# SSM forward and FFN gate/up of one training step: from one after the other to one interleaved phase

## The chip, the cores and the metric

The kernel runs on 1 core of one Trainium2 chip, in one launch. The metric is the device time of that core in microseconds (us), the median of 3 runs.

## The reference

One block, forward and backward, in bfloat16, L = 2048 positions, D = 576 channels, N = 128 states per channel, F = 4608 hidden units:

```python
xn = layernorm(x)                       # [2048, 576]
K  = Re(sum_n C*dt*B * exp(dt*A*l))     # one kernel of 2048 taps per channel
s  = irfft(rfft(xn) * rfft(K)) + xn * Dskip
h  = silu(xn @ w1) * (xn @ w3)          # [2048, 4608]
out = x + s * silu(h @ w2)
```

The outputs are `out` and the gradients of x, the eight SSM parameters and the three weight matrices for a given `grad_out`.

## The kernel before

The program is written phase by phase; the Tile framework's scheduler makes from that one fixed, in-order instruction list for each engine, taking ready work by priority, and the priority of an instruction is by default its place in the program. The DMA issues are instructions too: SP and ACT issue most of them, POOL the rest.

- **Layernorm and constants** (`phase1_layernorm`, `build_dft_mats`, `phase2_params`). Sixteen tiles of 128 positions are normalised into `xn_bf`, transposed by PE, and the transposed copy `xnT_bf` is written to `XNT_dram`. `phase2_params` makes the angles of the state rates, splits them into three bfloat16 parts and stores these to `PCS_dram`.
- **Kernel generation** (`phase2_kgen`, `kgen_chunk`, `trig`), 36 chunks of 16 channels. PE forms exponents (`e_ps`) and angles (`t_ps`) as small matmuls against a selector; ACT takes the Exp (`E_g`, six chunks as a group), DVE masks the angle to an integer (`m_k`), ACT takes Sin, Abs, Sin (`S_k`, `A_k`, `C_k`). DVE multiplies them (`q_k`, `p_k`), negates a part for the backward pass (`npi`), and stores `[3, a, d]` planes of it to `PZ_dram`. DVE then makes `t_k` and `v_k`, PE contracts 64 small matmuls into `kps`, and DVE casts these into `KT`.
- **Convolution** (`phase3_conv`, `conv_half`, `dft_block`, `cmul_acc`, `idft_tile`). For each half of the channels and four blocks of 512 positions: DFT of `KT` by PE (`dft_ps` to `kraw`, `k`, `kz`), DFT of `xn_bf` (to `u`), complex products on DVE (`cm_t`, `V`), inverse DFT (`inv_ps`), and on DVE the skip term (`xd`) and its sum (`s_t`), which goes to `S_dram`.
- **FFN hidden** (`phase4_hidden`). `xnT` comes back from `XNT_dram`. For each of 36 blocks of 128 hidden units and each half of 1024 positions, PE makes `pg` and `pu`, ACT takes Silu (`s_t`) and copies `u_t`, DVE copies `g_t` and makes `h_t`; `G_dram`, `U_dram`, `H_dram` receive them. `w2res`, all of w2 in SBUF, is loaded here on the POOL queue.
- **FFN out** (`phase4_output`): `hc` is read back from `H_dram`, PE multiplies with `w2res` into `po`.
- **Backward** (`phase5_ssm_bwd` and after). The part that the change touches is `param_chunk`, which for each of 36 chunks makes the same Exp, Sin and Cos again (`m_q`, `E_q`, `S_q`, `A_q`, `C_q`, `qi`, `qr`), contracts them with the gradient into `pT`, multiplies `pT` with the reloaded `pz` (`pr_q`, four instructions of 128x512) and reduces (`S_all`). Chunks are taken in pairs. After it come the gradients of the weights (phase 6).

The product with the reloaded planes is

```python
pz = tp_.tile([P, 3, LT, DC], BF16, name="pz")
nc.vector.tensor_tensor(out=pr[:, :, kind], in0=pT[:, :, :, kind * LT:(kind + 1) * LT],
                        in1=pz[:, s:s + 2].rearrange("p r a d -> p d r a"), op=ALU.mult)
```

so that its second operand is read with a step of 16 elements (32 bytes).

Of the kernel before, what the change touches and what calls it, by code (L numbers as in the profile page):

```python
# [60 lines left out]
class K:  # L61
# [58 lines left out]
    def phase1_layernorm(self):  # L120
        nc, cfg = self.nc, self.cfg
        L, D, LT, DT = cfg.L, cfg.D, cfg.LT, cfg.DT
        self.persist = self.ctx.enter_context(self.tc.tile_pool(name="persist", bufs=1))
# [8 lines left out]
        assert half <= 512 and D % 2 == 0
        with self.tc.tile_pool(name="ln_big", bufs=1) as big, self.tc.tile_pool(name="ln_sb", bufs=3) as sb, \
                self.tc.tile_pool(name="ln_small", bufs=4) as small, \
                self.tc.tile_pool(name="ln_ps", bufs=2, space=bass.MemoryType.PSUM) as ps:
            self.xnT_bf = big.tile([P, DT, L], BF16, name="xnT_bf")
            for i in range(LT):
                xt = sb.tile([P, D], BF16, name="xt")
                self.dma(xt[:], xf[i * P:(i + 1) * P, :])
# [10 lines left out]
                nc.vector.tensor_scalar(out=self.xn_bf[:, i, :], in0=xt[:], scalar1=self.rstd[:, i:i + 1],  # L150
                                        scalar2=self.negmr[:, i:i + 1], op0=ALU.mult, op1=ALU.add)
            if cfg.dch[-1][1] < P:
                nc.vector.memset(self.xnT_bf[cfg.dch[-1][1]:P, DT - 1, :], 0.0)
            TB = 8
            for c, (do, dsz) in enumerate(cfg.dch):
                for tb in range(0, LT, TB):
                    ntb = min(TB, LT - tb)
                    pt = ps.tile([P, TB * P], BF16, name="pt")
                    for j in range(ntb):
# [3 lines left out]
            for c in range(DT):
                self.dma(self.XNT_dram[:, c, :], self.xnT_bf[:, c, :])
            self.dbg_out("xn", self.xn_bf[:])
            self.dbg_out("xnT", self.xnT_bf[:])
            self.dbg_out("rstd", self.rstd[:])
            self.xnT_bf = None


# [128 lines left out]
    def trig(self, sb, m, nbits, n_el, tagp):  # L299
# [3 lines left out]
        A = sb.tile([P, n_el], FP32, name="A_" + tagp)  # L303
        nc.scalar.activation(out=A[:], in_=m[:], func=ACT.Abs, scale=2.0 ** -nbits, bias=self.nhalf_col[:])  # L304
        C = sb.tile([P, n_el], BF16, name="C_" + tagp)
        nc.scalar.activation(out=C[:], in_=A[:], func=ACT.Sin, scale=-6.283184, bias=self.halfpi_col[:])
# [1000 lines left out]
```

## Time and profile before

| what | us |
|---|---|
| median of 3 runs | 3076.25 |
| lowest and highest | 3070.47 and 3078.03 |
| the profiled execution | 3080.9 |
| its span in the trace | 3079.1 |
| PE busy in the span | 2130.0 (69%) |
| DVE busy | 1698.6 (55%) |
| ACT busy | 1387.4 (45%) |
| POOL busy | 256.2 (8%) |
| mean granted TensorE clock | 0.787 |

The span is what the trace covers; the execution's own time is 1.8 us longer. Busy shares are means over stages that lean on different engines, so the view to start from is the table of stages: for each stretch the busy time of each engine and the granted clock of PE. The chain of waits on the profile's page covers only the part from some 1076 us on.

### The profile page before, as it was taken

What the parts mean: (1) busy time and instruction counts of PE and PEld (TensorE: products, weight loads), DVE (VectorE), ACT (ScalarE), POOL (GpSimd) and SP (SyncE); (2) the same over time, 40 slices, a digit from 0 to 9 for tenths busy, and PEclk for the clock granted to TensorE, in tenths of its full rate; (3) what the DMA queues carried; (4) which work ended last, traced back from release to release, by engine and by line L of the source; (5) the groups of instructions that cost most, each with busy time, mean ns of one, the idle gap of its engine ahead of it and who ended that gap; (6) DMA issues with size and microseconds to landing.
All of it is one profiled execution on the core that took longest, in us unless ns stands there. A gap on an engine that the chain in (4) does not pass through costs nothing.

```text
span 3079.1 us, 41743 instructions
## 1 busy us (share of the span) xinstructions
PE 2130.0 (69%) x17026; PEld 1366.9 (44%) x17094; DVE 1698.6 (55%) x2604; ACT 1387.4 (45%) x1493; POOL 256.2 (8%) x505
## 2 busy tenths in 40 slices
PE   1466576499979855444444442598999999928999
PEld 0123255133337633221211111376777766716777
DVE  6668679544435578887777779343444433301222
ACT  3599952144431121226776773575556555400000
POOL 0000000111101100000000000122222222100000
PEclk8555578799989977765555555899999999968999
DMA  2200022567666423110000001754454444276442
GB/s 80 44 22 27 23 106 98 172 215 244 222 236 225 146 71 93 58 41 18 15 15 18 15 14 55 177 149 144 132 146 133 134 134 139 72 170 193 158 154 89
DMA packets 323652, 338.45 MB, mean 110 GB/s; under 512 B 114474, under 2 KB 282668, under 8 KB 320260
## 3 DMA queue, kind: packets, MB, share of 16 engines
q1 hardware_dynamic: 183516, 128.00, 14.4%
q0 software_dynamic: 33552, 109.15, 10.8%
q10 hardware_dynamic: 106392, 98.63, 10.3%
q8 instruction: 134, 2.20, 0.3%
q14 instruction: 58, 0.48, 0.1%
HBM read 166.30 MB, written 152.88 MB: 104 GB/s over the span
## 4 chain that ended last, share of the span: by engine, by line
PE 23%; DVE 16%; issue 8%; ACT 6%; DMA 6%; SPq 3%; POOL 2%; ACTq 0%; POOLq 0%; DVEq 0%
PE px L1189 9%; PE ph L1096 4%; DVE pr_q L906 4%; SPq L1001 3%; DMA out_dram<-gw 3%; PE pgw L1137 3%; ACT S_q L302 2%; PE pT L902 2%; DVE S_all L908 2%; PE pgw L1125 2%; ACT A_q L304 2%; DVE m_q L890 1%; DVE cm_t L524 1%; PE ptr L1009 1%; DMA w2T<-w2r 1%
## 5 line engine op out<-in xcount | busy, mean ns | idle before, releaser
L1189 PE MATMUL px<-w1T,ggc 128*128 128x288 bf16 x1152 | 237.1, 288 | 42.6 <-DMA w1T<-in_B_w_dram 42.6
L1189 PE MATMUL px<-w3T,guc 128*128 128x288 bf16 x1152 | 237.1, 288 | 33.8 <-DMA guc<-GU_dram 20.1
L1137 PEld LDWEIGHTS <-xn_bf 128*128 128x128 bf16 x2304 | 228.3, 100 | 67.7 <-issue 37.3
L1096 PE MATMUL ph<-go_oT,w2T 128*128 128x512 bf16 x682 | 162.3, 382 | 46.9 <-DMA go_oT<-GOT_dram 43.2
L1140 DVE CAST gw<-pgw 128x256 bf16<-128x256 f32 x144 | 59.9, 423 | 234.4 <-DMA out_dram<-gw 137.3
L661 DVE CAST g_t<-pg 128x1024 bf16<-128x1024 f32 x72 | 88.2, 1225 | 181.9 <-ACT s_t L660 181.9
L906 DVE TENSOR_TENSOR pr_q<-pT,pz 128x512 f32<-128x512 f32 x144 | 146.9, 1061 | 71.2 <-PE pT L902 71.2
L653 PEld LDWEIGHTS <-wmB_w 128*128 128x128 bf16 x1152 | 107.3, 98 | 167.2 <-issue 45.1
L1193 DVE TENSOR_TENSOR gx<-px,gx 128x288 f32<-128x288 f32 x32 | 13.2, 452 | 300.4 <-PE px L1189 300.4
L1206 ACT ACTIVATE t<-gx 128x576 f32<-128x576 f32 x16 | 10.9, 683 | 367.8 <-DVE gx L1193 367.8
L902 PE MATMUL pT<-gKK,qr 128*128 128x32 bf16 x576 | 69.7, 233 | 142.6 <-DVE qr L896 142.6
L1125 PE MATMUL pgw<-go_o,h_n 128*128 128x288 bf16 x1152 | 164.9, 286 | 0.9
L1137 PE MATMUL pgw<-gg_n,xn_bf 128*128 128x256 bf16 x1152 | 138.1, 282 | 34.2 <-DVE gw L1140 34.2
L697 PE MATMUL po<-w2res,hc 128*128 128x288 bf16 x1152 | 146.2, 289 | 17.6 <-DMA hc<-H_dram 17.6
L660 ACT ACTIVATE s_t<-pg 128x1024 bf16<-128x1024 f32 x72 | 73.8, 1024 | 162.6 <-PE pu L658 162.6
L653 PE MATMUL pg<-xnT,wmB_w 128*128 128x512 bf16 x561 | 137.5, 383 | 12.4 <-issue 11.6
L1189 PEld LDWEIGHTS <-ggc 128*128 128x128 bf16 x1152 | 113.5, 99 | 72.7 <-issue 43.4
L1189 PEld LDWEIGHTS <-guc 128*128 128x128 bf16 x1152 | 113.4, 99 | 64.2 <-DMA guc<-GU_dram 20.7
L653 PE MATMUL pu<-xnT,wmB_w 128*128 128x512 bf16 x562 | 137.0, 383 | 4.6 <-DMA wmB_w<-in_B_w_dram 3.9
L1137 PE MATMUL pgw<-gu_n,xn_bf 128*128 128x256 bf16 x1152 | 137.5, 273 | 0.0
L902 PEld LDWEIGHTS <-qr 128*128 128x128 bf16 x576 | 63.9, 122 | 164.6 <-DVE qr L896 164.6
L697 PEld LDWEIGHTS <-hc 128*128 128x128 bf16 x1152 | 112.5, 99 | 48.0 <-issue 18.1
(333 smaller groups left out, 4980.7 us busy)
## 6 DMA issues: line engine op xcount, KB each, us to landing
U_dram<-u_t POOLq DMA_DIRECT2D x36, 512.0 KB, 3.1
G_dram<-g_t POOLq DMA_DIRECT2D x36, 512.0 KB, 4.1
H_dram<-h_t SPq DMA_DIRECT2D x36, 512.0 KB
hc<-H_dram SPq DMA_DIRECT2D x8, 2304.0 KB
gate<-G_dram POOLq DMA_DIRECT2D x36, 512.0 KB, 4.5
up<-U_dram POOLq DMA_DIRECT2D x36, 512.0 KB, 6.5
GU_dram<-guT ACTq DMA_DIRECT2D x36, 512.0 KB
GG_dram<-ggT ACTq DMA_DIRECT2D x36, 512.0 KB
```

The source lines that it names most:

```text
L302: nc.scalar.activation(out=S[:], in_=m[:], func=ACT.Sin, scale=6.283184 / 2 ** nbits, bias=self.npi_col[:])
L653: nc.tensor.matmul(pt[:, o:o + 512], lhsT=wm[w][:, c, cs], rhs=xnT[:, c, t0:t0 + 512], start=(c == 0), stop=False)
L660: nc.scalar.activation(out=s_t[:, hs], in_=pg[:], func=ACT.Silu)
L661: nc.vector.tensor_copy(out=g_t[:, hs], in_=pg[:])
L697: nc.tensor.matmul(po_[:, pi_, 0:pw], lhsT=hc[:, fi, k * P:(k + 1) * P], rhs=self.w2res[:, fi, po:po + pw], start=(fi == 0), stop=(fi == F ...
L902: nc.tensor.matmul(pT[:, dl, k, :], lhsT=q[:, dl, :], rhs=gKK[:, :, :, d0 + dl], start=True, stop=True)
L906: nc.vector.tensor_tensor(out=pr[:, :, kind], in0=pT[:, :, :, kind * LT:(kind + 1) * LT], in1=pz[:, s:s + 2].rearrange("p r a d -> p d r a ...
L1001: self.nc.sync.dma_start_transpose(out=dst, in_=src)
L1096: nc.tensor.matmul(ph[:, q * 512:(q + 1) * 512], lhsT=w2T[:, c, :], rhs=go_oT[:, c, hh * HL + q * 512:hh * HL + (q + 1) * 512], start=(c = ...
L1125: nc.tensor.matmul(pgw[pi_][:, 0:pw], lhsT=h_ns[fl][:, tt, :], rhs=go_o[:, tt, po:po + pw], start=(tt == 0), stop=(tt == LT - 1))
L1137: nc.tensor.matmul(pw_[:, 0:GW], lhsT=self.xn_bf[:, tt, c * P:(c + 1) * P], rhs=nat[:, tt, :], start=(tt == 0), stop=(tt == LT - 1))
L1189: nc.tensor.matmul(px[pi_][:, 0:pw], lhsT=act[:, fi, k * P:(k + 1) * P], rhs=wT[:, fi, po:po + pw], start=(fi == 0 and ai == 0), stop=(fi ...
```

## The change

The SSM forward and the FFN hidden phase are put into the same stretch of the program, in SBUF and PSUM pools that don't overlap, and their order is set by hand: `at(us)` sets the scheduler's priority to a nominal time. Chunk `ch` of kernel generation has the time 8 x ch, the 16 steps of the convolution follow at 8 each, and hidden block `fi` has the time 12 x fi, so both end at a nominal 416 to 432. With that come these edits:

- `phase2_params` runs first, then layernorm (one Sqrt for all tiles; `xnT` stays in SBUF, `XNT_dram` is gone), then the DFT matrices.
- A new `ssm_early`, ahead of the merged phase, makes all 36 Exp tiles (`E_k`, one ACTIVATE of 128x1536 each) and all DFT blocks of `xn_bf`, and stores them to `E_dram` and `UH_dram`; the merged phase loads them again.
- In a chunk, `A_k` is written over `m_k`; the planes for `PZ_dram` are put into `[3, d, a]` order by two POOL instructions (128x512 and 128x256), where DVE had `npi`; the cast into `KT` goes from DVE to ACT.
- In the convolution `kraw` is bfloat16, its casts are per 288 columns, the skip term is three matmuls with a diagonal matrix (`dskip_diag`) that add into the inverse DFT's PSUM tile, and ACT copies the result; `xd` and the sum on DVE are gone.
- In the hidden phase PSUM tiles are 512 columns (144 steps of `pg` and `pu` in four banks), `g_t` is copied by DVE and ACT in turn, stores are of 1024 columns.
- w2 is loaded behind the hidden phase, as nine tiles, into SBUF that the merged phase's pools had.
- In `param_chunk`, `pz` is `[3, d, a]`, so that `pr_q` reads it in runs of 16 elements; its PSUM pool `b_ps` has 3 buffers for 2.

```diff
+    def at(self, us):
+        self.tc.cur_priority = 100000 + int(us * 1000)
...
+            for ch in range(NCH):
+                pe = ps.tile([P, TW], FP32, name="e_ps")
+                for o in range(0, TW, 512):
+                    nc.tensor.matmul(pe[:, o:o + 512], lhsT=LR_[0:48, ch, :], rhs=self.SELR[0:48, o:o + 512], start=True,
+                                     stop=True)
+                E = ep.tile([P, TW], BF16, name="E_k")
+                nc.scalar.activation(out=E[:], in_=pe[:], func=ACT.Exp)
+                nc.sync.dma_start(out=self.E_dram[ch], in_=E[:])
...
-        npi = sb.tile([P, AH, DC], BF16, name="npi")
-        nc.vector.tensor_scalar(out=npi[:], in0=p[:, 1, 0:AH, :], scalar1=-1.0, scalar2=None, op0=ALU.mult)
+        pz = sb.tile([P, 3, DC, AH], BF16, name="pz_k")
+        ph = p[:, :, 0:AH, :].rearrange("p r a d -> p r d a")
+        nc.gpsimd.tensor_copy(out=pz[:, 1:3], in_=ph)
+        nc.gpsimd.tensor_scalar(out=pz[:, 0], in0=pz[:, 2], scalar1=-1.0, scalar2=None, op0=ALU.mult)
...
-        nc.vector.tensor_copy(out=self.KT[:, :, d0:d0 + DC], in_=kps[:].rearrange("p d a -> p a d"))
+        nc.scalar.copy(out=self.KT[:, :, d0:d0 + DC], in_=kps[:].rearrange("p d a -> p a d"))
...
-                xd = spool.tile([P, W], FP32, name="xd")
-                nc.vector.tensor_tensor(out=xd[:], in0=self.xn_bf[:, t, cs], in1=self.dskip_row[:, cs], op=ALU.mult)
+                pt = ps.tile([P, 512], FP32, name="et_ps")
+                self.idft_tile(pt, V, oc, skip)
                 s_t = spool.tile([P, W], BF16, name="s_t")
-                nc.vector.tensor_tensor(out=s_t[:], in0=pt[:, 0:W], in1=xd[:], op=ALU.add)
+                nc.scalar.copy(out=s_t[:], in_=pt[:, 0:W])
...
+            self.at(T0 - 50)
+            w2 = []
+            for fi in range(0, FT, GRP):
+                w2g = wpool.tile([P, GRP, D], BF16, name=f"w2g{fi}")
+                nc.gpsimd.dma_start(out=w2g[:], in_=aps["B_w2"][fi * P:(fi + GRP) * P, :].rearrange("(c p) d -> p c d", p=P))
...
-        pz = tp_.tile([P, 3, LT, DC], BF16, name="pz")
+        pz = tp_.tile([P, 3, DC, LT], BF16, name="pz")
...
+        with tc.tile_pool(name="xT", bufs=1) as xp, tc.tile_pool(name="kg_sel", bufs=1) as selp:
+            k.SEL, k.SELR = k.build_selectors(selp)
+            k.phase1_layernorm(xp)
+            k.build_dft_mats(matp)
+            k.ssm_early(matp)
+            with tc.tile_pool(name="f_w", bufs=2) as wp, \
+                    tc.tile_pool(name="f_gu", bufs=3) as gup, \
+                    tc.tile_pool(name="f_ps", bufs=2, space=bass.MemoryType.PSUM) as fps:
+                k.ssm_forward(0, 8, 8)
+                k.ffn_hidden(wp, gup, fps, 0, 12)
+        k.ffn_output(480, 10)
+        k.at(700)
```

On ACT, at the start of kernel generation, the list of before runs through the trigonometry of the chunks with Exp and table loads between (`E_g` is the Exp of a later group):

```order
L382 ACTIVATE E_g<-e_ps 128x512 x18
L306 ACT_TABLE_LOAD
L306 ACTIVATE C_k<-A_k,halfpi_col 128x1536
L304 ACTIVATE A_k<-m_k,nhalf_col 128x1536
L302 ACTIVATE S_k<-m_k,npi_col 128x1536
L306 ACTIVATE C_k<-A_k,halfpi_col 128x1536
L304 ACTIVATE A_k<-m_k,nhalf_col 128x1536
L382 ACT_TABLE_LOAD
L382 ACTIVATE E_g<-e_ps 128x512
L306 ACT_TABLE_LOAD
```

The same place now, right behind the 36 Exp of `ssm_early`:

```order
L384 ACTIVATE E_k<-e_ps 128x1536 x36
L296 ACT_TABLE_LOAD
L296 ACTIVATE S_k<-m_k,npi_col 128x1536
L677 ACT_TABLE_LOAD
L677 ACTIVATE s_t<-pg 128x512
L298 ACTIVATE m_k<-m_k,nhalf_col 128x1536
L682 CAST u_t<-pu 128x512
L300 ACTIVATE C_k<-m_k,halfpi_col 128x1536
L677 ACTIVATE s_t<-pg 128x512
L681 CAST g_t<-pg 128x512
L682 CAST u_t<-pu 128x512
L677 ACTIVATE s_t<-pg 128x512
```

Silu of the hidden phase and Sin of the chunks now take turns, with one table load for each at the start and none between; 96 of the 144 `s_t` stand ahead of the last `C_k`, and 48 behind it, beside the convolution.

On POOL, where the FFN's own loads are issued, the w2 loads of before stand ahead of the stores of the hidden phase:

```order
L693 DMA s_t_8395<-S_dram 128x576
L638 DMA w2res<-in_B_w_dram 128x4x576 x9
L667 DMA U_dram<-u_t 128x2048
L666 DMA G_dram<-g_t 128x2048
L667 DMA U_dram<-u_t 128x2048
```

Now they stand at its end, and the first of them waits for PE's last matmul of the hidden phase, since its tile lies in SBUF of that phase:

```order
L723 DMA s_t_8984<-S_dram 128x576
L721 DMA x_t<-in_A_u_dram 128x576
L722 DMA go_t<-in_grad_out_dram 128x576
L723 DMA s_t_9095<-S_dram 128x576
L710 DMA w2g_8853<-in_B_w_dram 128x4x576
L687 DMA G_dram<-g_t 128x1024
L710 DMA w2g_8855<-in_B_w_dram 128x4x576
```

What moved is all nine loads, from before the first hidden block to behind the last.

On DVE, in the parameter sums, the list of one pair of chunks was (`m_q` masks an angle, `qi` and `qr` are the two products, `pr_q` and `S_all` the sums):

```order
L890 TENSOR_SCALAR m_q<-q_ps 128x512 x7
L896 TENSOR_TENSOR qi<-E_q,S_q 128x2048 x2
L896 TENSOR_TENSOR qr<-E_q,C_q 128x2048
L906 TENSOR_TENSOR pr_q<-pT,pz 128x16x32 x3
L908 TENSOR_REDUCE S_all<-pr_q 128x16x2
L906 TENSOR_TENSOR pr_q<-pT,pz 128x16x32
L908 TENSOR_REDUCE S_all<-pr_q 128x16x2
L896 TENSOR_TENSOR qr<-E_q,C_q 128x2048
L906 TENSOR_TENSOR pr_q<-pT,pz 128x16x32 x3
```

and is now:

```order
L920 TENSOR_SCALAR m_q<-q_ps 128x512 x7
L926 TENSOR_TENSOR qi<-E_q,S_q 128x2048 x2
L926 TENSOR_TENSOR qr<-E_q,C_q 128x2048 x2
L936 TENSOR_TENSOR pr_q<-pT,pz 128x16x32 x3
L938 TENSOR_REDUCE S_all<-pr_q 128x16x2
L936 TENSOR_TENSOR pr_q<-pT,pz 128x16x32 x2
```

The second `qr` moved ahead of the first chunk's products. ACT's list of a pair now takes both Sin, both Abs and both Cos together behind eight Exp, with two table loads, where before Exp stood between them, with four. Behind the parameter sums the lists of all engines are as before.

## Rows read from the trace of the kernel before

**Rows 1.** Stages: length; PE, PEld, DVE, ACT, POOL busy (x); granted clock; DMA share; GB/s.
```profile
0.00:110.00 110.00, 15.54 (x91) 9.17 (x93) 64.12 (x187) 27.48 (x44) 5.14 (x16) 0.71 0.34 79
110.00:404.00 294.00, 181.36 (x2390) 86.59 (x2389) 215.09 (x450) 279.55 (x265) 0.00 (x0) 0.50 0.09 24
404.00:592.00 188.00, 114.25 (x896) 83.43 (x896) 150.66 (x215) 47.13 (x68) 11.63 (x18) 0.81 0.34 121
592.00:912.00 320.00, 296.84 (x1411) 115.51 (x1440) 130.34 (x110) 141.30 (x146) 38.08 (x72) 0.96 0.67 225
...
1077.00:1366.00 289.00, 143.84 (x811) 91.45 (x812) 247.15 (x298) 52.16 (x107) 0.00 (x0) 0.72 0.24 70
1366.00:1892.00 526.00, 228.02 (x1441) 97.31 (x1440) 401.22 (x454) 369.86 (x315) 3.33 (x8) 0.50 0.06 17
```

**Rows 2.** Timeline of DVE: the first angle of kernel generation (start, us, instruction, idle before).
```profile
109.94 2.48 DVE L398 TENSOR_SCALAR m_k<-t_ps 128x512 int32<-128x512 int32 x4 [10.35 <-PE t_ps L397]
```

**Rows 3.** Costliest groups of 110 to 404 us: busy us, mean ns, idle before, releaser.
```profile
L398 DVE TENSOR_SCALAR m_k<-t_ps 128x512 int32<-128x512 int32 x108 | 70.6, 681 | 27.0 <-ACT A_k L304 16.6 <-PE t_ps L397 10.4
L424 PE MATMUL kps<-v_k,q_k 128*64 128x16 bf16 x2176 | 70.5, 204 | 57.3 <-DVE v_k L418 54.9
L397 PE MATMUL t_ps<-SEL,lhs_t 128*128 128x512 bf16 x106 | 59.5, 605 | 13.6 <-DVE m_k L398 12.2 <-issue 0.2
...
L306 ACT ACTIVATE C_k<-A_k,halfpi_col 128x1536 bf16<-128x1536 f32 x35 | 54.9, 1568 | 0.3
...
L404 DVE TENSOR_TENSOR q_k<-E_g,S_k 128x1024 bf16<-128x1024 bf16 x35 | 23.9, 684 | 8.5 <-ACT S_k L302 6.6 <-ACT E_g L382 2.0
...
L406 DVE TENSOR_TENSOR p_k<-E_g,S_k 128x512 bf16<-128x512 bf16 x35 | 14.6, 416 | 0.0
```

**Rows 4.** Costliest groups of 592 to 912 us, the FFN hidden phase.
```profile
L661 DVE CAST g_t<-pg 128x1024 bf16<-128x1024 f32 x72 | 88.2, 1225 | 181.9 <-ACT s_t L660 181.9
L660 ACT ACTIVATE s_t<-pg 128x1024 bf16<-128x1024 f32 x72 | 73.8, 1024 | 162.6 <-PE pu L658 162.6
L662 ACT CAST u_t<-pu 128x1024 bf16<-128x1024 f32 x72 | 72.4, 1006 | 0.0
```

**Rows 5.** Costliest groups on ACT of 1978 to 2711 us: casts of PSUM tiles of two sizes.
```profile
L1099 ACT CAST gh<-ph 128x512 bf16<-128x512 f32 x136 | 77.9, 588 | 88.1 <-PE ph L1096 88.1
...
L1129 ACT CAST gw<-pgw 128x288 bf16<-128x288 f32 x72 | 25.8, 415 | 23.6 <-PE pgw L1125 19.8 <-issue 3.8
```

**Rows 6.** Costliest groups of 404 to 592 us, the convolution.
```profile
L501 PE MATMUL inv_ps<-V,dC 128*128 128x288 bf16 x128 | 36.3, 317 | 50.0 <-DVE V L525 49.4 <-DVE s_t L588 0.5
...
L485 PE MATMUL dft_ps<-xn_bf,dC 128*128 128x288 bf16 x128 | 21.7, 287 | 0.0
...
L586 DVE TENSOR_TENSOR xd<-xn_bf,dskip_row 128x288 f32<-128x288 bf16 x32 | 13.9, 444 | 0.0
L588 DVE TENSOR_TENSOR s_t<-inv_ps,xd 128x288 bf16<-128x288 f32 x32 | 13.7, 447 | 10.6 <-DMA S_dram<-s_t 6.5 <-PE inv_ps L501 4.2
```

**Rows 7.** Timeline of PE: the last matmuls of the hidden phase, the first of FFN out.
```profile
893.88 0.39 PE L658 MATMUL pu<-xnT,wtail 64*128 64x512 bf16 x1
...
912.13 0.88 PE L697 MATMUL po<-w2res,hc 128*128 128x288 bf16 x3 [17.64 <-DMA hc<-H_dram]
```

**Rows 8.** Costliest groups on POOL, whole span: its one 512-column instruction of before.
```profile
L323 POOL IOTA ii<- 128x512 int32 x1 | 0.7, 653 | 0.0
```

**Rows 9.** Costliest groups of 1366 to 1892 us, the parameter sums.
```profile
L906 DVE TENSOR_TENSOR pr_q<-pT,pz 128x512 f32<-128x512 f32 x144 | 146.9, 1061 | 71.2 <-PE pT L902 71.2
L890 DVE TENSOR_SCALAR m_q<-q_ps 128x512 int32<-128x512 int32 x144 | 88.9, 676 | 1.9 <-DMA GXN_dram<-gx 1.9
...
L875 ACT ACT_TABLE_LOAD x34 | 43.6, 1283 | 0.6
```

**Rows 10.** Timeline of DVE, one pair of chunks of the parameter sums.
```profile
1609.49 1.23 DVE L896 TENSOR_TENSOR qi<-E_q,S_q 128x2048 bf16<-128x2048 bf16 x1 [2.33 <-ACT S_q L302]
...
1614.66 3.03 DVE L906 TENSOR_TENSOR pr_q<-pT,pz 128x512 f32<-128x512 f32 x3 [2.05 <-PE pT L902]
```

More of the change, by code (lines that the diff above doesn't have):

```diff
@@ L150, in phase1_layernorm @@
[L150 to L153, printed above, removed]
-            TB = 8
[L155 to L159, printed above, removed]
+                nc.vector.bn_aggr(mv[:, i, :], stats[:])
@@ new lines, in phase1_layernorm @@
+            sd = sb.tile([P, LT], FP32, name="sd")
+            nc.scalar.activation(out=sd[:], in_=mv[:, :, 1], func=ACT.Sqrt, bias=self.eps_col[:], scale=1.0)
+            nc.vector.reciprocal(out=self.rstd[:], in_=sd[:])
+            negmr = sb.tile([P, LT], FP32, name="negmr")
+            nc.vector.scalar_tensor_tensor(out=negmr[:], in0=mv[:, :, 0], scalar=-1.0, in1=self.rstd[:], op0=ALU.mult,
+                                           op1=ALU.mult)
+            for i in range(LT):
+                nc.vector.tensor_scalar(out=self.xn_bf[:, i, :], in0=xs[i][:], scalar1=self.rstd[:, i:i + 1],
+                                        scalar2=negmr[:, i:i + 1], op0=ALU.mult, op1=ALU.add)
@@ L160, in phase1_layernorm @@
+            TB = 8
+            for tb in range(0, LT, TB):
+                tsl = slice(tb * P, (tb + TB) * P)
+                for c, (do, dsz) in enumerate(cfg.dch):
+                    pt = ps.tile([P, TB * P], BF16, name="ln_pt")
+                    for j in range(TB):
                         nc.tensor.transpose(pt[:dsz, j * P:(j + 1) * P], self.xn_bf[:, tb + j, do:do + dsz],
                                             self.ident_bf[:])
-                    nc.scalar.copy(out=self.xnT_bf[:dsz, c, tb * P:(tb + ntb) * P], in_=pt[:dsz, 0:ntb * P])
@@ L163, in phase1_layernorm @@
[L163 to L168, printed above, removed]
+                    if c % 2 == 0:
+                        nc.scalar.copy(out=self.xnT[:dsz, c, tsl], in_=pt[:dsz, :])
+                    else:
+                        nc.vector.tensor_copy(out=self.xnT[:dsz, c, tsl], in_=pt[:dsz, :])
@@ L302, in trig @@
         nc.scalar.activation(out=S[:], in_=m[:], func=ACT.Sin, scale=6.283184 / 2 ** nbits, bias=self.npi_col[:])
[L303 to L304 removed]
+        A = m[:].bitcast(FP32)
+        nc.scalar.activation(out=A, in_=m[:], func=ACT.Abs, scale=2.0 ** -nbits, bias=self.nhalf_col[:])
         C = sb.tile([P, n_el], BF16, name="C_" + tagp)
[L306 removed]
+        nc.scalar.activation(out=C[:], in_=A, func=ACT.Sin, scale=-6.283184, bias=self.halfpi_col[:])
         return S, C
@@ L660, in phase4_hidden @@
-                    nc.scalar.activation(out=s_t[:, hs], in_=pg[:], func=ACT.Silu)
-                    nc.vector.tensor_copy(out=g_t[:, hs], in_=pg[:])
-                    nc.scalar.copy(out=u_t[:, hs], in_=pu[:])
+                            nc.tensor.matmul(pt[:], lhsT=wm[w][:, c, cs], rhs=xnT[:, c, t0:t0 + 512], start=(c == 0),
+                                             stop=False)
+                    nc.tensor.matmul(pg[:], lhsT=wt[0:rem, cs], rhs=xnT[0:rem, nfull, t0:t0 + 512], start=False, stop=True)
@@ L663, in phase4_hidden @@
+                    nc.tensor.matmul(pu[:], lhsT=wt[rem:P, cs], rhs=xnT[rem:P, nfull, t0:t0 + 512], start=False, stop=True)
+                    nc.scalar.activation(out=s_t[:, qs], in_=pg[:], func=ACT.Silu)
+                    if q % 2 == 0:
+                        nc.vector.tensor_copy(out=g_t[:, qs], in_=pg[:])
+                    else:
+                        nc.scalar.copy(out=g_t[:, qs], in_=pg[:])
+                    nc.scalar.copy(out=u_t[:, qs], in_=pu[:])
                 nc.vector.tensor_tensor(out=h_t[:], in0=s_t[:], in1=u_t[:], op=ALU.mult)
-                nc.sync.dma_start(out=self.H_dram[:, :, fi, :].rearrange("c p l -> p c l"),
+                nch = HL // self.TC4
```

313 lines of the change are left out of this document (159 added, 154 removed).

## The prediction

> **What bounds the kernel now.** I read the table of stages first, since the shares of the whole span mix stages with different limits, then the costliest groups within the stages that the change touches, then short timelines where one stage hands over to the next. In the table [rows 1] kernel generation takes 294 us with ACT busy for 279.6 of them: ACT bounds it (95%). In the convolution, 188 us, DVE is busy for 150.7 (80%). In the FFN hidden phase, 320 us, PE is busy for 296.8 (93%), and DVE and ACT for 130 and 141 only. Three neighbouring stages, each with another engine as its bound, 802 us in all: whoever runs them side by side is limited by sums, not by the three bounds one behind the other. The fourth stage of interest is the parameter sums, 526 us, where DVE is busy for 401 and ACT for 370, so neither is full and waits between them count.
>
> **Ahead of the merged phase.** Kernel generation starts its first angle at 110 us [rows 2]. The new stage puts the 36 Exp of 128x1536 ahead of it. No row shows them; C_k, an ACTIVATE of the same 128x1536, takes 1568 ns [rows 3], so 36 x 1.57 = 57 us on ACT. Beside them PE makes three exponent matmuls per chunk (0.6 us each at the half clock, by t_ps in rows 3) and the DFT blocks of xn_bf, moved from the convolution, 256 matmuls of 128x288 at 287 ns [rows 6] = 73 us. If PE keeps up, ACT sets 57 us; if PE stays slow, 36 x 1.8 + 73 = 138 us. The list puts most DFT matmuls between the exponents, dense work, so I take ACT's value, plus 11 us for the last DFT blocks and the first angles: start at 110 + 57 + 11 = **178 us** (bounds 160 and 259). That layernorm and the parameters change places I put at nothing: the 10.35 us that DVE idles ahead of the first angle [rows 2] get cover, but lhs_r then queues on SP behind sixteen tile loads.
>
> **The merged phase**, engine by engine.
> - *ACT.* A chunk has Sin, Abs and Sin of 1.57 us and the cast into KT, taken as 0.42 by the 128x288 cast of 415 ns [rows 5]: 5.1 us, x 36 = 184. A step of 512 columns has one Silu and one u_t at 0.59 each (the 128x512 cast, rows 5) and g_t in every second step: 1.47 us, x 144 = 212, where s_t and u_t took 146 before [rows 4]: smaller tiles and half of g_t cost ACT 66 us. The convolution's 64 half casts and 32 s_t at 0.415 are 40. Sum 436. Exp and the table loads between are gone from here.
> - *DVE.* A chunk: three m_k of 0.681, four multiplications of 0.684, four of 0.416 [rows 3], 6.4 us, x 36 = 232. A step: half a g_t of 0.68 (m_k's 512 columns) and half an h_t of 0.68 (q_k's 128x1024): 0.68 us, x 144 = 98. Convolution: 150.7 less xd and s_t, 27.6 [rows 6]: 123. Sum 453.
> - *PE.* From 592 to 893.9 us [rows 1, 7] 1440 matmuls of 512 columns took 302, 2.1 us a step. t_ps and kps are 59.5 + 70.5 us at the half clock [rows 3], between 65 and 130 now, I take 90. The convolution's 114 lose the 43 of xn_bf [rows 6] and gain 96 skip matmuls, by inv_ps at 0.317 at most 30: about 85. Sum 477.
>
> The three are nearly equal, so none can idle for long, and the order decides. By the list, 96 of the 144 steps stand ahead of the last Cos. So the first part is bound by ACT, 184 + 96 x 1.47 = 325, and the second by PE, 85 + 48 x 2.1 = 186: **511 us** with no wait at all. For the waits I divide by the share that the bound engine reaches in the stages of now: 95% (ACT, kernel generation), 93% (PE, hidden), 85% (DVE, 247 of 289 us in the stage from 1077), 80% (DVE, convolution), 76% (DVE, parameter sums) [rows 1]. With three engines that hand tiles to each other in a fixed order I take 91%: 511 / 0.91 = 562 us. The hidden phase then ends at 178 + 562 = **740 us**, where its last matmul now stands at 894 [rows 7]: **-154 us**.
>
> *Queues.* The phase moves what the hidden phase and the convolution moved, 225 x 320 and 121 x 188 us [rows 1], 95 MB, less w2, and 14 MB of E read back: some 104 MB in 562 us, 185 GB/s, below the 225 of now. On SP the loads of E stand between H stores that wait for h_t; three E tiles are two chunks, 31 us, of cover. On POOL the copies for PZ_dram wait for p_k, and G and U stores stand behind them; three buffers of g_t and u_t, two of them four steps of work ahead, cover that. I put all of it at nothing, and it costs a PE wait per store if the cover is gone (the packing rival).
>
> **Handover to FFN out.** Now 18 us pass from the last matmul to the first po, and that wait is for hc [rows 7], behind H's store. The nine w2 tiles, 5.3 MB, then come at the same time on the same engines instead of long before. At the 225 GB/s of the hidden phase [rows 1] they take 24 us. Nothing if they hide in hc's wait, 24 if all is added; the po matmuls need the tiles one after another, so I take **+10**.
>
> **Parameter sums**, 36 chunks in 18 pairs, 526 / 18 = 29.2 us a pair. *Order:* with both qr ahead of the products, one of the two waits of 2.05 us for pT [rows 10] has cover; with the Sin, Abs, Cos paired, two table loads of 1.28 us [rows 9] go from ACT, but the first qr now comes later; I count -1 us a pair, between 0 and -3. *The product:* pr_q takes 1061 ns, m_q, also 512 columns out of PSUM, 676 [rows 9]. Against it pr_q reads one more operand; s_t, with two operands and 288 columns, takes 447, and by the same slope (the two m rows and s_t) a contiguous product of 512 would take about 0.68. So 0.385 us of each is left for its access pattern. If the 32-byte step of pz is the cause, eight per pair give -3.1 us; if PSUM's pieces or the f32 output are, 0. I take the whole, since a step is what sets this product apart from s_t. Of the Trainium skill, "SBUF — State Buffer" (Specifications (TRN2)) says that each access which crosses to a new 16-byte line pays a penalty. By that the gain would be the whole 3.1 us a pair; no row here shows it alone. Together 4 us x 18 = **-70** (bounds 0 and -110). The stage between, from 1077, and all behind keep their lists: nothing.
>
> **Sum**, against the profiled execution of 3080.9: -154 + 10 - 70 = -214, so 2867; it stood 4.6 us above the median, so about **2862 us**.
>
> **The rivals.**
> - *pr_q doesn't get faster.* What is left is the order, -18 instead of -70: 2862 + 52 = 2914. For it: pT is read in pieces in both kernels. 14%.
> - *POOL blocks DVE.* The trace before has hardly any POOL arithmetic; a 128x512 instruction took 0.65 us [rows 8], so copy and negation are at least 1 us a chunk, and I allow 3. If DVE stood still for them, 36 x 1 to 36 x 3 = 36 to 108 us would fall on DVE, most of it on the first part, where it has 232 + 65 = 297 against ACT's 325. With 72 DVE has 369, and (369 - 325) / 0.91 = 48 us are added: 2910. In a sentence of its own: the Trainium skill, "GPSIMD Engine Reference" (8. Key points), says that GpSimd shares its SBUF interfaces with VectorE, and that instructions of DVE with two SBUF inputs contend; the chunk's multiplications are such ones, and no run here shows it yet. 8%.
> - *The phases don't pack.* Four PSUM tiles for the FFN and four for the SSM are few buffers; if one chain waits while the other holds the in-order engine, the share falls to the 76% of the parameter sums: 511 / 0.76 = 672, the end at 850, -44 + 10 - 70: 2972. Nearly the same comes out if nothing overlaps at all: 195 (ACT alone at 95%) + 123 / 0.8 + 320 = 669. 16%.
> - *It packs as well as the best stage.* 511 / 0.95 = 538, the end at 716: 2838, or less if the start is at 160. 11%.
> - *The clock stays low (slower).* With PE busy for 62% and 43%, in kernel generation and the parameter sums, the granted clock was 0.50, its 1.2 GHz level; in the hidden phase, 93%, 0.96 [rows 1]. If the SSM's pauses in PE's list hold it at 0.50 in the merged phase, the FFN's 302 us become 580, with the 130 of kernel generation and 85 x 1.6 = 137 of the convolution 847 of PE, at 93% 911. The end is at 1089, +195 + 10 - 70 = +135: 3211 us. It turns slower than before below a granted clock of about 0.6, where PE alone takes the merged phase beyond 770 us. Against it: PE has 477 of 562 us, 85%, and in the convolution 61% went with 0.81 [rows 1]. 6%.
>
> **How the numbers follow.** The forecast, 2862, has 45%; its own range is 2815 to 2915, by a packing of 87 to 95%, a start at 160 to 200 and w2 at 0 to 24. The low end of the whole range, 2770, is tight packing with an early start and the parameter sums at their bound; the high end, 3000, is the phase that doesn't pack with w2 at its bound. Left out are the low clock and what lies beyond both ends, under 2 in 10. A measurement of this kernel tells some 0.3%, 9 us, from no change. All cases but the last are faster; between packing at 76% and the low clock lies a thin strip of no change: faster 0.92, same 0.02, slower 0.06.
>
> **What would show it.** *Start:* the first S_k of the merged phase at 170 to 200 us, the 36 E_k at about 1.57 us each with ACT hardly idle; if E_k waits for e_ps, PE was slow. *Merged phase:* ACT the busiest up to the last C_k at some 530 us, PE behind it, a granted clock of 0.9 or so throughout, the last pu matmul near 740. If DVE's q_k, p_k and t_k last longer than the 684 and 416 ns of rows 3, POOL is in the way; if no engine is over 80% busy, the waits have it. *Handover:* the first po some 25 to 30 us after the last pu, released by a w2 tile. *Parameter sums:* pr_q near 0.68 us and a stage of some 455 us; at 1.06 us the stage stays over 500 and the sum was 50 us too good. The prediction is wrong as a whole if the merged phase lasts over 670 us, which means that two of the engines took turns rather than ran together.

## The result, and the profile after

The changed kernel takes **2835.47 us** (four runs, 2834.8 to 2836.38) against 3077.14 for the kernel before on the same chips (four runs, 3070.47 to 3083.27): a ratio of 0.9215, 95% interval 0.9196 to 0.9235. The prediction was 2862, its range 2770 to 3000. The span of the profiled execution went from 3079.1 to 2833.8 us, by 245.3.

Where they went is read from the first and last starts of a few groups in both traces, for the hidden phase from the end of its last matmul:

| stretch | before, us | after, us | difference | forecast |
|---|---|---|---|---|
| start to the end of the last hidden matmul | 894.5 | 722.6 | -171.9 | -154 |
| from there to the first po | 17.6 | 19.9 | +2.3 | +10 |
| first po to last po | 157.1 | 165.5 | +8.4 | 0 |
| last po to the first m_q | 297.7 | 300.2 | +2.5 | 0 |
| parameter sums, first m_q to last S_all | 524.8 | 451.9 | -72.9 | -70 |
| last S_all to the first px | 857.5 | 848.8 | -8.7 | 0 |
| first px to the last gx | 323.1 | 318.4 | -4.7 | 0 |

The table of stages of the changed kernel (length; PE, PEld, DVE, ACT and POOL busy; granted clock, DMA share, GB/s), to be read against [rows 1]:

```profile
0.00:108.00 108.00, 32.30 (x165) 18.74 (x166) 64.32 (x171) 18.50 (x24) 6.54 (x18) 0.85 0.26 64
108.00:200.00 92.00, 90.30 (x262) 27.31 (x261) 14.38 (x19) 53.98 (x38) 0.00 (x0) 0.50 0.45 180
200.00:215.00 15.00, 11.29 (x39) 5.48 (x39) 4.63 (x7) 0.68 (x1) 0.00 (x0) 0.50 0.57 194
215.00:541.00 326.00, 297.76 (x3292) 131.91 (x3327) 290.11 (x484) 292.39 (x384) 141.73 (x170) 0.97 0.63 206
541.00:714.00 173.00, 168.03 (x1053) 88.27 (x1069) 147.13 (x182) 96.72 (x209) 27.27 (x49) 1.00 0.55 191
```

In the fourth line PE, DVE and ACT are each busy for 290 to 298 of 326 us: three engines near 90% at once, which no stage of before had. In the fifth PE alone is the bound, at 97%. The second line is the surprise: PE is busy for 90 of 92 us and yet at a granted clock of 0.50, the 1.2 GHz level, while ACT, for which this stage was sized, is busy for 54. The timeline of ACT there shows Exp waiting for PE (start, us, instruction, idle before it and what ended it):

```profile
113.31 1.45 ACT L384 ACTIVATE E_k<-e_ps 128x1536 bf16<-128x1536 f32 x1 [0.55 <-PE e_ps L381]
116.02 1.45 ACT L384 ACTIVATE E_k<-e_ps 128x1536 bf16<-128x1536 f32 x1 [1.26 <-PE e_ps L381]
118.30 1.45 ACT L384 ACTIVATE E_k<-e_ps 128x1536 bf16<-128x1536 f32 x1 [0.83 <-PE e_ps L381]
```

One Exp every 2.5 us in place of every 1.45, so the merged phase starts at 215 us:

```profile
L384 ACT ACTIVATE E_k<-e_ps x36: 1446/1450/1450, 110.0 to 197.9; 128x1536 bf16<-128x1536 f32 x36
L296 ACT ACTIVATE S_k<-m_k,npi_col x36: 1567/1596/1652, 215.4 to 534.8; 128x1536 bf16<-128x1536 int32 x36
L300 ACT ACTIVATE C_k<-m_k,halfpi_col x36: 1576/1586/1666, 221.3 to 539.6; 128x1536 bf16<-128x1536 f32 x36
L677 ACT ACTIVATE s_t<-pg x144: 578/597/661, 218.9 to 722.6; 128x512 bf16<-128x512 f32 x144
```

(A line gives the shortest, median and longest duration in ns and the first and last start in us.) Within the merged phase the costliest groups show a second thing that was only a rival: DVE's products are slow while POOL reorders the planes (busy us, mean ns, idle before):

```profile
L450 POOL COPY pz_k<-p_k 128x512 bf16<-128x512 bf16 x35 | 48.3, 1380 | 45.6 <-DVE p_k L446 45.3
...
L451 POOL TENSOR_SCALAR pz_k<-pz_k 128x256 bf16<-128x256 bf16 x35 | 37.4, 1069 | 2.3
L456 DVE TENSOR_TENSOR t_k<-p_k,nWiT 128x1024 bf16<-128x1024 bf16 x35 | 37.3, 1065 | 0.0
L456 DVE TENSOR_TENSOR t_k<-p_k,WrT 128x1024 bf16<-128x1024 bf16 x35 | 35.5, 1014 | 0.3
...
L444 DVE TENSOR_TENSOR q_k<-E_l,S_k 128x1024 bf16<-128x1024 bf16 x36 | 27.1, 752 | 8.1 <-ACT S_k L296 8.1
```

t_k and q_k are of one shape. Before, q_k took 684 ns [rows 3] and t_k as much:

```profile
L415 DVE TENSOR_TENSOR t_k<-p_k,WrT 128x1024 bf16<-128x1024 bf16 x36 | 24.6, 685 | 0.4
L415 DVE TENSOR_TENSOR t_k<-p_k,nWiT 128x1024 bf16<-128x1024 bf16 x36 | 24.6, 683 | 0.0
```

t_k, which runs while POOL copies, takes 1014 and 1065 now. POOL's copy is drawn out as well, to anything between 1098 and 2712 ns:

```profile
L450 POOL COPY pz_k<-p_k x36: 1098/1116/2712, 224.8 to 542.3; 128x512 bf16<-128x512 bf16 x36
```

In the parameter sums pr_q [rows 9] and its neighbours are:

```profile
L936 DVE TENSOR_TENSOR pr_q<-pT,pz x144: 677/680/692, 1224.1 to 1659.3; 128x512 f32<-128x512 f32 x144
...
L938 DVE TENSOR_REDUCE S_all<-pr_q x72: 1207/1209/1214, 1225.9 to 1660.1; 128x32 f32<-128x1024 f32 x72
```

### The profile page after: what moved, and what is told of

The parts are those of the page before. It is cut to its first block, busy times and chain, and to the rows that moved or that the text cites. A ratio compares the mean times of both kernels' runs of the same rounds, so it can differ in the third digit from the quotient of the medians.

```text
span 2833.8 us, 42478 instructions
## 1 busy us (share of the span) xinstructions
PE 2127.6 (75%) x17097; PEld 1348.5 (48%) x17190; DVE 1606.1 (57%) x2512; ACT 1319.3 (47%) x1633; POOL 389.1 (14%) x655
## 3 DMA queue, kind: packets, MB, share of 16 engines
q10 hardware_dynamic: 98552, 93.80, 10.7%
## 5 line engine op out<-in xcount | busy, mean ns | idle before, releaser
L727 PE MATMUL po<-w2g,hc 128*128 128x288 bf16 x1152 | 149.0, 292 | 25.1 <-DMA hc<-H_dram 20.0
L673 PE MATMUL pg<-xnT,wmB_w 128*128 128x512 bf16 x538 | 156.6, 388 | 10.1 <-DVE g_t L679 7.8
L673 PE MATMUL pu<-xnT,wmB_w 128*128 128x512 bf16 x559 | 158.9, 386 | 1.5 <-issue 0.5
L1094 POOL DMA_DIRECT2D gate<-G_dram x36 | 19.3, 538 | 877.2 <-PE sT_ps L951 769.2
L919 PE MATMUL q_ps<-rt,SELB 4*128 4x512 bf16 x144 | 80.0, 580 | 72.4 <-DVE m_q L920 70.3
L1126 PEld LDWEIGHTS <-w2T 128*128 128x128 bf16 x720 | 69.0, 98 | 119.7 <-DMA out_dram<-gl_bf 38.6
L1129 ACT CAST gh<-ph 128x512 bf16<-128x512 f32 x144 | 82.3, 587 | 90.2 <-PE ph L1126 90.2
```

What stands on the lines that cost most here:

```text
L673: nc.tensor.matmul(pt[:], lhsT=wm[w][:, c, cs], rhs=xnT[:, c, t0:t0 + 512], start=(c == 0), stop=False)
L727: nc.tensor.matmul(po_[:, pi_, 0:pw], lhsT=hc[:, fi, k * P:(k + 1) * P], rhs=w2[fi][:, po:po + pw], start=(fi == 0), stop=(fi == FT - 1))
L919: nc.tensor.matmul(pt[:], lhsT=SELB[0:4, :], rhs=rt[0:4, o:o + 512], start=True, stop=True)
L1126: nc.tensor.matmul(ph[:, q * 512:(q + 1) * 512], lhsT=w2T[:, c, :], rhs=go_oT[:, c, hh * HL + q * 512:hh * HL + (q + 1) * 512], start=(c = ...
L1129: nc.scalar.copy(out=gh[:, hh * HL:(hh + 1) * HL], in_=ph[:])
```

## The experiments

Ten kernels were run, in three sets. The first asks what the two large terms are made of, and what the slow DVE and the low clock cost; the second follows up; the third puts together what gained.

**The step of pz put back** (e1_step_back).

```diff
...
-        pz = tp_.tile([P, 3, DC, LT], BF16, name="pz")
+        pz = tp_.tile([P, 3, LT, DC], BF16, name="pz")
...
-                                        in1=pz[:, s:s + 2].rearrange("p r d a -> p d r a"), op=ALU.mult)
+                                        in1=pz[:, s:s + 2].rearrange("p r a d -> p d r a"), op=ALU.mult)
```

> The changed kernel with the planes back in [3, a, d] order, so that pr_q reads pz in steps of 32 bytes again; the two POOL instructions stay and copy without reordering. Theory (the step was what pr_q paid for): pr_q goes from 0.68 us back to about 1.06, the parameter sums gain 18 x 8 x 0.38 = 55 us, the time is about 2890. Rival (pr_q got faster for another reason, such as the order around it or the third PSUM buffer): pr_q stays at 0.68 and the time at 2835.

Measured: 2871.43 us (0.9336 of before, 0.9318 to 0.9354). The two groups of the parameter sums:

```profile
L936 DVE TENSOR_TENSOR pr_q<-pT,pz x144: 1046/1060/1131, 1210.3 to 1701.0; 128x512 f32<-128x512 f32 x144
...
L938 DVE TENSOR_REDUCE S_all<-pr_q x72: 1202/1210/1227, 1213.3 to 1702.2; 128x32 f32<-128x1024 f32 x72
```

pr_q is back at 1.06 us, and first m_q (1194.4) to last S_all takes 507.8 us, 56 more than the 451.9 of the changed kernel: the step was what pr_q paid for. The total rose by 36 only, since the merged phase got 13 us shorter (last s_t at 709.3 in place of 722.6). POOL's copy without reordering takes 863 ns in the mean in place of 1372 (609 at the shortest in place of 1098), and t_k 765 and 949 ns: the first sign that DVE's slowness costs time.

**One chain after the other** (e2_one_after_other).

```diff
-                    tc.tile_pool(name="f_ps", bufs=2, space=bass.MemoryType.PSUM) as fps:
                 k.ssm_forward(0, 8, 8)
-                k.ffn_hidden(wp, gup, fps, 0, 12)
+                with tc.tile_pool(name="f_ps", bufs=2, space=bass.MemoryType.PSUM) as fps:
+                    k.ffn_hidden(wp, gup, fps, 430, 12)
...
```

> The changed kernel with the PSUM pool of the hidden phase opened only when the SSM's pools are closed, and with later priorities, so that the two chains run one after the other; all other edits stay. Theory (the overlap is the gain of the forward part): kernel generation alone some 190 us by ACT, the convolution some 130 to 150 by DVE, the hidden phase some 310 by PE, 640 in place of 508: about 2965. Rival (the gain came from the work that was taken out, such as Exp in one piece, no table loads, no skip term on DVE): no more than 30 us are lost, about 2865.

Measured: 2997.28 us (0.9737, 0.9716 to 0.9757), 162 more than the changed kernel.

```profile
L296 ACT ACTIVATE S_k<-m_k,npi_col x36: 1559/1578/1578, 204.1 to 423.3; 128x1536 bf16<-128x1536 int32 x36
...
L677 ACT ACTIVATE s_t<-pg x144: 597/597/598, 579.3 to 887.5; 128x512 bf16<-128x512 f32 x144
```

The last s_t starts at 887.5 us, where it started at 894.5 before. So all other edits of the forward part together are worth 7 us: kernel generation (some 224 us for 294) and convolution (149 for 188) are shorter, but the new early stage gives it back, since the first Sin is at 204 where the first angle was at 110 [rows 2]. The overlap is nearly the whole gain of the forward part, 162 of some 172 us.

**The planes on DVE** (e3_planes_dve).

```diff
-        nc.gpsimd.tensor_copy(out=pz[:, 1:3], in_=ph)
-        nc.gpsimd.tensor_scalar(out=pz[:, 0], in0=pz[:, 2], scalar1=-1.0, scalar2=None, op0=ALU.mult)
+        nc.vector.tensor_copy(out=pz[:, 1:3], in_=ph)
+        nc.vector.tensor_scalar(out=pz[:, 0], in0=pz[:, 2], scalar1=-1.0, scalar2=None, op0=ALU.mult)
```

> The changed kernel with the reordering copy and the negation on DVE in place of POOL. In the changed kernel's trace t_k took 1.01 and 1.07 us where it took 0.68 before, with POOL busy for 2.4 us in each chunk. Theory (POOL slows DVE's two-operand instructions, but DVE has room): t_k is back at 0.68, DVE saves 30 us and pays 36 x (0.5 to 1.1 + 0.22) = 26 to 47, and the time stays within 10 us of 2835. Rival (the slowed DVE sets the merged phase): more than 10 us faster. Second rival (t_k is slow for another reason, PSUM or ACT traffic): t_k stays at 1.0 us and the time rises by 30 or more.

Measured: 2837.18 us (0.9222, 0.9204 to 0.924), no difference from the changed kernel that can be told.

```profile
L456 DVE TENSOR_TENSOR t_k<-p_k,nWiT 128x1024 bf16<-128x1024 bf16 x35 | 24.1, 689 | 0.0
...
L450 DVE COPY pz_k<-p_k 128x512 bf16<-128x512 bf16 x35 | 22.1, 631 | 0.2
```

With no POOL arithmetic t_k is back at 0.69 us, so POOL was the cause; DVE pays 0.63 + 0.23 us a chunk for doing the work itself, 31 us, about what it saves. The run shows the cause but not the price, because both kernels carry the work.

**The planes left out** (e7_no_planes) give the price.

```diff
-        pz = sb.tile([P, 3, DC, AH], BF16, name="pz_k")
-        ph = p[:, :, 0:AH, :].rearrange("p r a d -> p r d a")
-        nc.gpsimd.tensor_copy(out=pz[:, 1:3], in_=ph)
-        nc.gpsimd.tensor_scalar(out=pz[:, 0], in0=pz[:, 2], scalar1=-1.0, scalar2=None, op0=ALU.mult)
-        nc.sync.dma_start(out=self.PZ_dram[:, ch], in_=pz[:])
+        dst = self.PZ_dram[:, ch].rearrange("p r d a -> p r (d a)")
+        nc.sync.dma_start(out=dst[:, 1:3], in_=p[:, :, 0:AH, :].rearrange("p r a d -> p r (a d)"))
+        nc.sync.dma_start(out=dst[:, 0], in_=p[:, 1, 0:AH, :].rearrange("p a d -> p (a d)"))
```

> The changed kernel without the two POOL instructions of a chunk: the planes go to DRAM as they stand, neither reordered nor negated (the reordering and the sign are left out of the computation); the layout of pz and the read of pr_q stay. Theory (POOL's hold on DVE costs the merged phase part of the 30 us by which t_k, q_k and v_k were lengthened): t_k back at 0.68, the merged phase 10 to 25 us shorter, 2810 to 2825. Rival (DVE has room): 2835.

Measured: 2810.49 us (0.9134, 0.9117 to 0.9151), 25 less. The first part of its merged phase:

```profile
216.00:520.00 304.00, 296.55 (x3325) 130.42 (x3324) 258.97 (x483) 287.21 (x384) 54.56 (x100) 0.99 0.71 220
```

304 us in place of 326: DVE does 31 us less, and PE now reaches 98%. A rival is POOL's queue, since G and U stores stand behind the copies; but e3 takes the copies out of that queue too, and with DVE's load as before it gained nothing. So DVE did not have room, though no view of the changed kernel shows it as the bound: with all three engines near 90%, time put on DVE came out in the total. For PE and ACT no run tried the same.

**The planes late** (e8_planes_late) uses that, on top of e4 (below): DVE negates as before, the planes are stored in [3, a, d] order, and POOL reorders in the parameter sums.

```diff
...
+        pz0 = tp_.tile([P, 3, LT, DC], BF16, name="pz0")
+        self.dma(pz0[:], self.PZ_dram[:, ch])
         pz = tp_.tile([P, 3, DC, LT], BF16, name="pz")
-        self.dma(pz[:], self.PZ_dram[:, ch])
+        nc.gpsimd.tensor_copy(out=pz[:], in_=pz0[:].rearrange("p r a d -> p r d a"))
```

> The 128-row exponent matmuls, and the planes as in the kernel before (negated by DVE, stored in [3, a, d] order); the reordering is one POOL instruction of 768 columns per chunk in the parameter sums instead, between the load of pz and pr_q. Theory (POOL's work is better placed where DVE mostly reads PSUM): the merged phase 10 to 20 us shorter, the parameter sums at 452 to 460, the time about 2770 to 2780. Rival (POOL lengthens qi, qr there as much, or pr_q waits for it): 2786 or more.

Measured: 2770.43 us (0.9002, 0.8983 to 0.902), 16 less than e4. The POOL instruction takes 1.57 us a chunk, the parameter sums last from 1141.7 to the last S_all at 1595.0, 453.3 us against 452.0 in e4, and qi and qr keep their 1.23 us: there it is nearly free.

**Exponents over 128 rows** (e4_rows128).

```diff
+            nc.vector.memset(LR_[:], 0.0)
...
-                    nc.tensor.matmul(pe[:, o:o + 512], lhsT=LR_[0:48, ch, :], rhs=self.SELR[0:48, o:o + 512], start=True,
+                    nc.tensor.matmul(pe[:, o:o + 512], lhsT=LR_[:, ch, :], rhs=self.SELR[:, o:o + 512], start=True,
```

> The changed kernel with the exponent matmuls of the early stage over all 128 rows (zero weights in rows 48 to 127) in place of 48; same columns, same results. From 108 to 200 us PE was busy for 90 of 92 us at a granted clock of 0.50, and ACT waited for it. Theory (the clock stayed low because half of these matmuls use few rows of the array): the clock rises to 1.0 in this stretch, the 36 Exp take about 55 us instead of 90, and the time is about 2800. Rival (it stays low for the short changing matmuls whatever their rows): clock 0.50, no change, 2835.

Measured: 2786.54 us (0.9057, 0.9039 to 0.9075), 49 less than the changed kernel.

```profile
108.00:180.00 72.00, 60.25 (x326) 31.64 (x331) 24.52 (x37) 59.56 (x47) 0.00 (x0) 0.99 0.77 296
...
L385 ACT ACTIVATE E_k<-e_ps x36: 1444/1469/1519, 109.9 to 158.8; 128x1536 bf16<-128x1536 f32 x36
```

The same columns, 80 rows of zeros more, and the granted clock is 0.99 in place of 0.50; the 36 Exp take 50 us, at ACT's own rate, and the first Sin is at 171. PE is idle here for 12 of 72 us, and the clock stays up all the same.

**Only the DFT blocks without their wait** (e10_one_bank), to see whether it is the rows or the pauses.

```diff
...
-                        pt = psu.tile([P, 2, 512], FP32, name="u_ps")
                         for ri, mat in enumerate((self.dC, self.dSf)):
+                            pt = psu.tile([P, 512], FP32, name="u_ps")
...
-                        nc.vector.tensor_copy(out=u[:, :, kt, :], in_=pt[:, :, 0:W])
+                            nc.vector.tensor_copy(out=u[:, ri, kt, :], in_=pt[:, 0:W])
```

> The changed kernel with 48-row exponent matmuls as they were, and only the DFT blocks of xn_bf in one-bank PSUM tiles of their own, two of them, so that PE no longer waits 0.85 us for the cast of each block. Theory (full rows raise the clock, the 48-row matmuls hold it down): the clock is 1.0 from about 85 to 107 us, where only DFT blocks run, and back at 0.50 once the exponents are mixed in; the 36 Exp still take 80 us or more, time 2815 to 2835. Rival (what kept the clock low were the waits for the cast just before): once risen it stays at 1.0, the 36 Exp take 55 us, 2785 to 2795.

Measured: 2808.14 us (0.9117, 0.9084 to 0.9149), but the four runs lie between 2792.48 and 2817.8, which no other kernel here shows. The windows of the profiled one (2816.78 us):

```profile
84.00:88.00 4.00, 3.88 (x26) 2.63 (x25) 2.54 (x7) 0.00 (x0) 0.00 (x0) 0.85 0.42 41
...
104.00:108.00 4.00, 4.00 (x24) 1.75 (x24) 1.75 (x4) 3.60 (x4) 0.00 (x0) 1.00 0.89 352
...
112.00:116.00 4.00, 3.33 (x16) 1.16 (x15) 0.82 (x2) 3.98 (x4) 0.00 (x0) 0.99 0.99 403
116.00:120.00 4.00, 4.00 (x14) 1.53 (x14) 0.92 (x2) 2.66 (x2) 0.00 (x0) 0.50 0.69 278
...
150.00:160.00 10.00, 10.00 (x30) 3.12 (x29) 1.83 (x4) 5.80 (x4) 0.00 (x0) 0.50 0.38 153
```

DFT blocks alone raise the clock at 85 us; with 48-row exponents mixed in from 94 us on it holds for 22 us, falls at 116, and stays at 0.50, with PE busy all the time, until the exponents end at 170. So both forecasts fell in part: the 48-row mix doesn't pull the clock down at once, but it doesn't bring it back either. Two pauses of PE, 0.36 and 0.31 us for ACT, stand just ahead of the fall, so what ended the high clock there is not shown; pauses alone didn't end it in e4. When it falls is likely what spreads the runs: the two shorter ones have a mean granted clock of 0.848, the two longer 0.838 and 0.841. One trace can't show more.

**The order of the parameter sums undone** (e5_abs_tile): Abs gets a tile of its own again there, by which the instruction lists take the order of before.

```diff
-        A = m[:].bitcast(FP32)
+        A = sb.tile([P, n_el], FP32, name="A_" + tagp)[:] if tagp == "q" else m[:].bitcast(FP32)
```

> The changed kernel with Abs of the parameter sums written to a tile of its own again (A_q) in place of over m_q. In its instruction lists the order of a pair of chunks is then that of the kernel before (Exp between the Sin and Cos, second qr behind the first products); nothing else differs. Theory (the order is worth about 1 us a pair): the parameter sums take 452 + 18 = 470 us and the time is about 2853. Rival (the order is worth nothing, the whole 73 us are the product's): 452 us, 2835.

Measured: 2852.52 us (0.9266, 0.9238 to 0.9294), 17 more. First m_q at 1207.9, last S_all at 1678.0: 470.1 us, 18 more than the 451.9. The edit that made the order is the Abs in place, not the third PSUM buffer of b_ps, which is still there. What the order moves are DVE's waits; the first two lines are the changed kernel's, the last two this run's:

```profile
L926 DVE TENSOR_TENSOR qr<-E_q,C_q 128x2048 bf16<-128x2048 bf16 x36 | 44.1, 1225 | 89.3 <-ACT C_q L300 89.3
L936 DVE TENSOR_TENSOR pr_q<-pT,pz 128x512 f32<-128x512 f32 x144 | 92.1, 681 | 2.5 <-PE pT L932 1.3
...
L936 DVE TENSOR_TENSOR pr_q<-pT,pz 128x512 f32<-128x512 f32 x144 | 92.5, 684 | 71.3 <-PE pT L932 71.3
L926 DVE TENSOR_TENSOR qr<-E_q,C_q 128x2048 bf16<-128x2048 bf16 x36 | 43.9, 1220 | 11.3 <-ACT C_q L300 11.3
```

**The early stage in another form** (e6_early_exp): on top of e4, exponents written ahead of layernorm, and the DFT blocks in one-bank tiles.

```diff
...
-            k.phase1_layernorm(xp)
-            k.build_dft_mats(matp)
-            k.ssm_early(matp)
+            with ExitStack() as st:
+                k.ssm_early_exp(st)
+                k.phase1_layernorm(xp)
+                k.build_dft_mats(matp)
+                k.ssm_early_dft()
```

> The 128-row exponent matmuls, and the early stage in another form: the exponents are written ahead of layernorm in the program, and each DFT block of xn_bf has a PSUM tile of one bank of its own with its own cast, so that PE doesn't wait for the 0.76 us cast of a two-bank tile. Theory (with the clock at 1.0, ACT's 36 Exp are all that is left, 52 us): the first Sin at 150 to 160 us in place of 171, the time 2770 to 2780. Rival (the start is set by the parameters and layernorm, which now share DVE and SP): at or above the 2786.5 of the 128-row kernel.

Measured: 2749.16 us (0.8931, 0.8912 to 0.895), 37 less than e4 and beyond the forecast: the first Exp is at 71 us, right behind the DFT matrices on ACT, and the first Sin at 138. Of the 39 us by which the first Exp is earlier, 27 are ACT's wait for e_ps, which in e4 stood behind nine DFT blocks on PE and is gone here; 12 are the DFT matrices, done at 70 us in place of 81, with layernorm's loads ahead of most of the parameters' stores on SP. What the one-bank tiles add was not taken apart.

**Both variants** (e9_both): the edits of e6 and e8 in one kernel.

> The early stage in its other form (exponents ahead of layernorm, 128 rows, one-bank DFT tiles) and the late reordering of the planes together, the two variants that gained so far. Theory (they gain in different stretches, the first 38 us before the merged phase, the second 16 within it and behind): 2749 - 16 = 2733. Rival (the earlier start is given back in the merged phase): 2745 to 2750.

Measured: **2726.01 us** (0.8854 of before, 0.8841 to 0.8866), the fastest version here, 109 us below the changed kernel.

```profile
138.00:436.00 298.00, 292.67 (x3315) 129.35 (x3313) 263.62 (x519) 285.88 (x384) 54.57 (x100) 0.99 0.71 220
```

The gains add up: 2733 was expected, and the 7 us beyond it are no more than the spread of the runs of e6 or of this kernel, 7 us each. In the first part of the merged phase PE is at 98%: what is left there is PE's own work.

## Why the prediction was right, and where it was not

- **The stage table's argument**, three bounds side by side in place of one behind the other, held: e2 puts the overlap at 162 us, and without it the hidden phase ends 7 us from where it ended before.
- **The start**, 178 us, failed: 215. The step that failed is "dense work, so I take ACT's value". PE was dense, and at the 1.2 GHz level all the same, so PE set the pace: 89 us for the Exp in place of 57. The slow PE had been written down, at 138 us, and put aside because dense work was taken to raise the clock. e4 puts the price at 49 us; with the clock up, ACT's Exp take 50 us and the first Sin is at 171, so the rest of the term was sound to 7 us.
- **The merged phase**, 562 us, took 507 (215.4 to 722.6). The step that failed is the 511 us without waits. It adds durations, and consecutive instructions of an engine overlap in the trace by some 0.1 us: in [rows 10] three pr_q, of 1.06 us each by [rows 9], take 3.03 us together. ACT's sum for the first part was 325, its busy time is 292. Busy times, which count an overlap once, give 292 for ACT and 298 for PE in the first part and 168 of 173 for PE in the second. The share of 91% came from busy times [rows 1] and was laid on a sum of durations; laid on the busy times, (292 + 168) / 0.91 gives 505, near the 507 measured.
- The two errors, +37 and -55, have opposite signs, so the end of the hidden phase (723 for 740) looks better than its working.
- **POOL blocks DVE** had 8%, and 48 us at 72 us of hold. It happened: t_k shows it, e3 names POOL, and e7 prices the planes at 25 us. The Trainium skill, "GPSIMD Engine Reference" (8. Key points), says that instructions of DVE with two SBUF inputs contend with GpSimd; the trace agrees for t_k (685 and 683 ns to 1014 and 1065) and for the q_k made from Sin (684 to 752; the one from Cos, which meets no POOL work, stays at 685), and m_k, which reads PSUM, keeps its 0.68 us. The rival's arithmetic failed in its condition: it asked whether DVE passes ACT, and with three engines near 90% none needs to pass.
- **Handover**, +10 for w2: the wait for the first po grew by 2.3 us, and it was for hc as before; the row of po says why more came behind it: after hc it waited twice for w2, 5.2 us in all, and the whole stage took 8.4 longer. The granted clock was 0.53 from 754 to 761 us, behind the longer of the two waits, and the po matmuls took 149.0 us in place of 146.2. The sum of both stretches, 10.7, is near the forecast's 10 by another split, so the match is partly luck.

```profile
L727 PE MATMUL po<-w2g,hc x1152: 285/286/448, 742.5 to 908.0; 128*128 128x288 bf16 x192
its engine sat idle before it (us, times) until:
  DMA hc<-H_dram: 20.0, 1
  DMA w2g<-in_B_w_dram: 5.2, 2
```

- **Parameter sums**, -70: -72.9. Both halves were right: the product -56 by e1 (forecast -55), the order -18 by e5 (forecast -18). That the order came out to the microsecond is partly luck, since the forecast took 1 us a pair from a range of 0 to 3: both waits of pr_q for pT went, 71 us to 1, where one was counted, and qr's wait for Cos grew from 11 us to 89 (the lines at e5). The Trainium skill, "SBUF — State Buffer" (Specifications (TRN2)), says that each crossing to a new 16-byte line pays a penalty; 1060 ns against 680 for the same product, with the 32-byte step and without, agrees.
- **Nothing behind**: the two stretches of the weight gradients are 8.7 and 4.7 us shorter with the same lists. In the traces of e1, e2 and e3 the first of them lasts 842 to 848 us as well, so it is no chance of the changed kernel's one trace, though the kernel before has one trace only; the cause was not tried and stays open.

## What to carry to other kernels

Where neighbouring stages are bound by different engines, add up each engine's busy time over both and compare the largest sum with the two lengths: that is the room, and a fixed order in disjoint buffers reached 90% and more of it. Then every engine is near its bound, so look for time that one engine takes from another, even where no view shows the one that loses it as the bound. Price a stage with matmuls at both clock levels, and trust neither until a trace of that mix of matmuls shows one.

## What the runs showed of the hardware

- A stretch in which PE was busy for 98% of the time stayed at a granted clock of 0.50 with 51.9 us of matmuls over 48 rows mixed with 47.9 us over 128 (108 to 200 us of the changed kernel), and was at 0.99 with the same matmuls over 128 rows, 80 of them zero (e4). At the high clock a mix with 48 rows held for 22 us, then fell and stayed low until the mix ended (e10). Matmuls over 64 rows, 75 us of the first part of the merged phase, went with a granted clock of 0.97 there.
- POOL took 1372 ns in the mean to copy 128x512 bfloat16 elements in a new order (1098 at the shortest) and 863 (609) in the old one, DVE 631 in the new one; the negation of 128x256 took 1072 ns (862) on POOL and 228 on DVE. The means on POOL likely hold waits for DVE: in e8, where the copy stands in the parameter sums, 128x768 took 1560 to 1572 ns each time.
- Sin and Silu took turns on ACT through the merged phase, 36 chunks and 144 steps, with no table load between them.
